# First sequence of an FNet + squared-ReLU kernel: E folded into Q's matmul group, small table loads on GpSimd's DMA queue, a new order of TensorE's opening

## The chip, the cores and the metric

The kernel runs on one core of a Trainium2 chip. The metric is the device time of one execution in microseconds (us); the number quoted for the kernel is the median of five runs, 1951.87 us (1948.48 to 1954.81). The profile is of one of these executions, whose own time is 1951.87 us and whose span, from the first to the last recorded instruction, is 1950.1 us.

## What is computed

Eight sequences of 3008 rows and 256 columns go through a two-dimensional Fourier transform of which only the real part is kept; the result, seen as 24064 tokens, goes through a small feed-forward block with a squared ReLU.

```python
X = np.fft.fft(x, axis=1)              # x: (8, 3008, 256) float32
X = np.fft.fft(X, axis=2)
t = X.real.astype(np.float32).reshape(8 * 3008, 256)
h = t @ w_in                           # w_in: (256, 2048)
r = np.maximum(h, 0.0)
out = (r * r) @ w_out                  # w_out: (2048, 256)
```

## The kernel before

**Two halves for each sequence.** For a sequence b the kernel first makes three matrices from the rows: P (128 x 1505, the cosine part of columns 0 to 127), Q (127 x 1505, the sine part of columns 1 to 127) and E (the cosine part of column 128, one row of 1505 values, which is wanted on all 128 partitions). Then, for blocks of 251 positions (`CK`) and for each of 8 steps j (`NJ`), `front` multiplies P by G1 and Q by G2 (L565, L566), adds E times a column gE and forms a sum and a difference on VectorE (L568 to L571), `combine` squares on ScalarE (L580, L581), and `back` multiplies by w_out (L605 or L618). G1, G2 and gE are products of the cosine and sine tables of the columns (`cosd`, `sind`) with w_in; `begin_win(j)` makes them for step j.

**How P, Q and E are made.** `load_x` brings seven tiles t of a sequence; `fold` adds and subtracts rows and columns on VectorE (`f_s`, `f_d`, `f_sc`, `f_dc`, `f_w`: L368 to L398), once for the cosine half (called `for_p`) and once for the sine half (`for_q`). `dft_ops` then has one group of five parts for each matrix and each parity kp of the output position: `even_n` (matmuls of tiles 0 to 3 into a tile of the pool `psd`, and a copy `da` on ScalarE, L475), `join_4` and `join_2` (VectorE, into `db` and `dc2`), `odd_n` (matmuls of tiles 4 to 6) and `join_1` (VectorE, into P, Q or E). Line L467 holds all these matmuls, L480 to L484 all the joins (the helper `both`). The pool `psd` has two buffers, and so has `psh`, which holds the first sequence's `odd_n` and later `front`'s products. The tables `cosT` and `sinT` are brought by `load_table` in 13 transfers each, of which ten are small (22 to 95 KB, the tiles 0 to 3) and three large (353 to 377 KB, the tiles 4 to 6).

**The first sequence (b = 0)** has no earlier work to hide in, so its order is written out by hand at L729 to L781: each call appends to the in-order queues of the engines. `groups_at` names the parts by number: P is 0 to 4 (kp 0) and 5 to 9 (kp 1), E is 10 to 14 and 15 to 19, Q is 20 to 24 and 25 to 29. For E, `even_n` and `odd_n` run the column broadcast to 128 columns, so that E comes out on all partitions at once. `awake(n)` issues n matmuls of the identity that nothing reads. `rounded(j)` is the last part of the conversion of w_in for step j (w_in comes as 64-bit numbers, which VectorE and ScalarE take apart: L241 to L254), `win[j][1]` the products into G1 and G2 (L269, L270), `win[j][2]` the matmul for gE (L278), and `copy_e` the copy into gE (L280).

**For the other sequences** E is computed once, in sequence 1's share of side work: seven rows, stored to the DRAM tile `e_dram` (L548) and read back by `load_e(b)`, broadcast over 128 partitions (L552).

**The DMA queues.** SyncE's queue (SP) issues nearly all transfers in program order; its rows in the trace are called SPq. Up to eight transfers are outstanding; an issue waits for the landing of the one eight before it, and for the instruction that frees or writes its buffer. ScalarE's queue issues three transfers, the tables `cosd` and `sind` (L739). GpSimd (POOL) issues none. In the main loop `weights()` appends for step i, among others, the load of w_in for step i + 3 (`begin_win(i + 3)`, whose transfers are issued by L226 on SP and whose first instruction on VectorE is L241).

Of the kernel before, what the change touches and what calls it, by code (L numbers as in the profile page):

```python
# [12 lines left out]
PSUM = bass.MemoryType.PSUM  # L13
P = 128
R = 32

# [63 lines left out]
def kernel(  # L82
# [12 lines left out]
    nc = tc.nc  # L95
# [72 lines left out]
    G2 = const.tile([P, F], F32, name="G2")  # L168
    gE = const.tile([P, NFC], F32, name="gE")

    def load_table(tab, src, tiles):

        for t in tiles:
            c, r0, step, rows = TILES[t]
            for i, (s0, count) in enumerate(row_tiles(S)):
                mine = [r for r in range(count) if (s0 + r - r0) % step == 0 and 0 <= (s0 + r - r0) // step < rows]
                if mine:
                    o, m = (s0 + mine[0] - r0) // step, len(mine)
                    while m % 15 and m % 16 and o + m < P and mine[0] + step * m < P:
                        m += 1  # L180
                    nk = NC[0][c]
                    nc.sync.dma_start(out=tab[o:o + m, :, PLACE[t]:PLACE[t] + nk],
                                     in_=src[mine[0]:mine[0] + step * (m - 1) + 1:step, :, i, 0:nk])

    make_identity(nc, ident)
    ramp = const.tile([P, 2], F32, name="ramp")
    nc.vector.memset(ramp[:, 0:1], 1151.0)
    nc.vector.memset(ramp[:, 1:2], 255.0 * 2.0 ** 23)
# [71 lines left out]
    def begin_win(j):  # L260

        w = ep.tile([P, 2, CH], F32, name="win", tag="sB" if j % 2 else "sA")
        finish = convert(parts(w, 1), win.pop(j, None) or load(pair_in(j)))

        def products():
            for tab, G, nm in ((cosd, G1, "mC"), (sind, G2, "mD")):
                pg = psm.tile([P, CH], F32, name="pg", tag=nm)
                for i in range(2):
                    nc.tensor.matmul(pg, tab[:, i], w[:, i], start=i == 0, stop=i == 1)  # L269
                nc.scalar.copy(G.rearrange("p (h j f) -> j p h f", h=2, j=NJ)[j],  # L270
                               pg.rearrange("p (h f) -> p h f", h=2))

        def for_e():

            ps = psd.tile([P, CH], F32, name="pe", tag="d")
            for h in range(2):
                fc = j + NJ * h
                nc.tensor.matmul(ps[:, h:h + 1], G2[:, fc * P:(fc + 1) * P], ident[:, P - 1:], start=True, stop=True)  # L278

            return lambda: nc.vector.tensor_scalar_mul(gE[:, j::NJ], ps[:, 0:2], 0.5)  # L280

        win[j] = finish, products, for_e
# [48 lines left out]
    NE = B - 1  # L331
    xe = const.tile([P, 4, NT, NE], F32, name="xe")
    we = const.tile([P, 2, NT, NE], F32, name="we")
    e_dram = dp.tile([NE, NKT], F32, name="e_dram")
    nc.gpsimd.memset(xe, 0.0)

    def load_column(t):
# [14 lines left out]
    def fold(b, t):  # L352
# [42 lines left out]
        def f_w(part=slice(0, D)):  # L395
            v, w = st["sc"], w_of(t)
            for kp in range(2):
                tt(out=w[r, kp, part], in0=v[r, 0, part], in1=v[r, 1, part], op=ALU.subtract if kp else ALU.add)  # L398

        if b == 0:  # L400
            return [f_s, f_d, f_sc, f_dc, lambda: f_w(PART[0]), lambda: f_w(PART[1])]
        ops = [(0.9, f_s), (0.9, f_d), (0.7, f_sc), (0.6, f_dc), (1.1, f_w)]
        if not odd or t == ODD0:
            return ops, None
# [42 lines left out]
    def dft_ops(b):  # L447
# [2 lines left out]

        def start():
            PQE[b] = [pq.tile([n, NKT], F32, name=nm, tag=nm)
                      for nm, n in (("Pt", P), ("Qt", P - 1), ("Et", P))]

        def group(kp, which):
            n = NE if b is None else P - 1 if which == 1 else P
            tab = sinT if which == 1 else cosT
            n2, _, n1, n0 = NC[kp]
            st = {}

            def product(ps, c):
                ts = [t for t in range(NT) if TILES[t][0] == c]
                for t in ts:
                    rows = TILES[t][3]
                    w = we[0:rows, kp, t] if b is None else folded[b, t][0:rows, kp, PART[which % 2]]
                    w = w[:, H:H + 1].to_broadcast([rows, n]) if which == 2 and b is not None else w[:, 0:n]
                    nc.tensor.matmul(ps, w, tab[0:rows, kp, PLACE[t]:PLACE[t] + NC[kp][c]],  # L467
                                     start=t == ts[0], stop=t == ts[-1])

            def even_n():  # L470
                st["ps"] = psd.tile([P, 512], F32, name="pd", tag="d")[0:n]
                a = st["a"] = hp.tile([P, 2 * P], F32, name="da", tag="da", bufs=2)[0:n]
                for c, at, nk in ((0, 0, n2), (1, n2, n2), (2, 2 * n2, n1)):
                    product(st["ps"][:, at:at + nk], c)
                nc.scalar.copy(a[:, 0:n2], st["ps"][:, 0:n2])  # L475

            def both(lo, hi, a, ps):

                nk, nh = a.shape[-1], hi.shape[-1]
                tt(out=lo, in0=a, in1=ps, op=ALU.add)  # L480
                if which == 1:
                    tt(out=hi[:, ::-1], in0=ps[:, 0:nh], in1=a[:, 0:nh], op=ALU.subtract)
                else:
                    tt(out=hi[:, ::-1], in0=a[:, 0:nh], in1=ps[:, 0:nh], op=ALU.subtract)  # L484
# [8 lines left out]
                st["c"] = hp.tile([P, NC[0][3]], F32, name="dc2", tag="dc2", bufs=2)[0:n, 0:n0]  # L493
                both(st["c"][:, 0:n1], st["c"][:, n1:n0], a, ps[:, 2 * n2:2 * n2 + n1])

            def odd_n():

                pool, tag = (psh, "h") if b == 0 else (psd, "d")
                ps = pool.tile([P, 512], F32, name="pd", tag=tag)[0:n]
                st["odd"] = ps[:, 0:n0]  # L500
                if not b:
                    return product(ps[:, 0:n0], 3)
                nq = (n0 + 2) // 2 if kp else (n0 + 1) // 2
# [25 lines left out]
                else:  # L529
                    tt(out=o[:, 1::2], in0=a[:, 1:nq], in1=ps[:, 1:nq], op=ALU.subtract)  # L530

            def join_1():
                dst = PQE[1][2][0:n] if b is None else PQE[b][which]
                nh = S // 8
                both(dst[:, kp:kp + 2 * n0 - 1:2], dst[:, M - kp - 2 * (nh - 1):M - kp + 1:2], st["c"],
                     st["odd"])

            ops = [(0.1, even_n), (0.4, join_4), (0.5, join_2), (0.1, odd_n), (0.8, join_1)]
            if b and kp:
                ops.insert(4, (0.5, join_odd))  # L540
            return ops

        ops = [] if b is None else [(0.0, start)]
        for which in (2,) if b is None else (0, 1) if b else (0, 2, 1):
            for kp in range(2):
                ops += group(kp, which)
        if b is None:
            ops.append((0.0, lambda: nc.sync.dma_start(out=e_dram[:, :], in_=PQE[1][2][0:NE])))  # L548
        return ops

    def load_e(b):
        nc.sync.dma_start(out=PQE[b][2], in_=e_dram[b - 1:b].to_broadcast([P, NKT]))  # L552


    def front(b, k0, n, j, between):
# [4 lines left out]
        for h in range(2):  # L560
            fc = j + NJ * h
            fs = slice(fc * P, (fc + 1) * P)
            ps = psh.tile([P, 2, CH], F32, name="ph", tag="h")
            hP, hQ = ps[:, 0, 0:n], ps[:, 1, 0:n]
            nc.tensor.matmul(hP, G1[:, fs], pt[:, ks], start=True, stop=True)  # L565
            nc.tensor.matmul(hQ, G2[0:P - 1, fs], qt[:, ks], start=True, stop=True)  # L566
            t = hp.tile([P, CK], F32, name="he", tag="he")[:, 0:n]
            nc.vector.scalar_tensor_tensor(out=t, in0=et[:, ks], scalar=gE[:, fc:fc + 1], in1=hP,  # L568
                                           op0=ALU.mult, op1=ALU.add)
            tt(out=g[:, h, 0, 0:n], in0=t, in1=hQ, op=ALU.add)  # L570
            tt(out=g[:, h, 1, 0:n][:, ::-1], in0=t, in1=hQ, op=ALU.subtract)  # L571
            between()
# [152 lines left out]
    def rounded(j):  # L725
        win[j][0]()
# [8 lines left out]
    for_p(1)  # L735
    begin_win(0)
    load_x(0, 2)
    for dst, src in ((cosd, cos_d), (sind[:, :, 0:P - 1], sin_d), (sind[:, :, P - 1:], alt_d)):
        nc.scalar.dma_start(out=dst, in_=src.rearrange("(c p) m -> p c m", p=P))  # L739
    load_x(0, 3)  # L740
    load_x(0, 4)
    load_table(cosT, cos_s, (0,))
    load_x(0, 5)
    load_table(cosT, cos_s, (1,))
    load_x(0, 6)
    load_table(cosT, cos_s, range(2, NT))
    load_table(sinT, sin_s, range(ODD0, NT))
    win[1] = load(pair_in(1))
    load_table(sinT, sin_s, range(ODD0))
    win[2] = load(pair_in(2))  # L750
    for_p(2)
    rounded(0)
    win[0][1]()
    awake(10)
    for_p(3)
    groups_at(0, 5)
    awake(12)
    for_q(1)
    for_p(4)
    for_p(5)  # L760
    for_q(2)
    for_p(6)
    groups_at(3, 8, 1, 2)
    for_q(4)
    groups_at(6, 7)
    for_q(5)
    groups_at(10, 15, 4)
    for_q(6)
    groups_at(9, 13, 18, 11, 12, 16, 17, 14)
    awake(4)  # L770
    groups_at(23)
    begin_win(1)
    groups_at(19, 28)
    copy_e = win[0][2]()
    for_q(3)
    groups_at(20, 25)
    awake(10)
    begin_win(2)
    rounded(1)
    groups_at(21, 22, 24, 26, 27, 29)  # L780
    copy_e()  # L781
    LAG = 2
    BLOCKS = [(k0, min(CK, NKT - k0)) for k0 in range(0, NKT, CK)]
    steps = [(b, k0, n, j) for b in range(B) for k0, n in BLOCKS for j in range(NJ)]
# [136 lines left out]
```

## Time and profile before

| | us |
|---|---|
| median of five runs (lowest to highest) | 1951.87 (1948.48 to 1954.81) |
| profiled execution | 1951.87 |
| its span | 1950.1 |
| TensorE (PE) busy in the span | 1937.2 (99%) |
| VectorE (DVE) busy | 1398.7 (72%) |
| GpSimd (POOL) busy | 1171.3 (60%) |
| ScalarE (ACT) busy | 924.3 (47%) |
| PE busy, first 68 us | 60.2 |
| PE busy, from 110 us to the end (1840 us) | 1835.1 |

Columns of the timeline: start and length in us, engine, line of the kernel, operation, tile written and tiles read, shape, number of records, and in brackets the idle time before it and what ended it. A matmul of float32 stands as two records. PEclk in a table of windows is the mean clock that the chip granted to TensorE, 1.00 being full. "Busy" for PE includes the time in which a matmul runs at a lower clock.

### The profile page before, as it was taken

Reading aid. Unit: us, or ns where it says so; the run is one execution under the profiler, and the core shown is the slowest. Engines: PE = TensorE matmul, PEld = TensorE weight load, DVE = VectorE, ACT = ScalarE, POOL = GpSimd, SP = SyncE. Lnnn points to the kernel's source line nnn. Section 1 sums busy time; section 2 is a strip of 40 time slices with the busy share of each in tenths; the row PEclk is TensorE's granted clock in tenths of the full one; section 3 lists DMA queues with packets and bytes.
Section 4 is the critical chain, followed back from the end, with each engine's and each line's share of the span. In section 5 each row is a group of like instructions: output and inputs, shape, how many; then the busy total and the mean of one; then the engine's idle time right before and its main releaser. Section 6 shows DMA issues by size and latency. Waiting matters only on the chain.

```text
span 1950.1 us, 27794 instructions
## 1 busy us (share of the span) xinstructions
PE 1937.2 (99%) x9296; PEld 1724.4 (88%) x9296; DVE 1398.7 (72%) x3442; ACT 924.3 (47%) x1068; POOL 1171.3 (60%) x1705
## 2 busy tenths in 40 slices
PE   8999999999999999999999999999999999999998
PEld 7888888888988889888988889888898888988887
DVE  8898967777677766777667776677767777655654
ACT  1754544455444544445444444444544454444443
POOL 0037746676567665666557665666756676566655
PEclk9999999999999999999999999999999999999999
DMA  7332102111011101111011100121002101100101
GB/s 210 98 45 52 33 10 53 33 27 29 14 45 35 39 16 27 41 35 33 12 35 38 44 19 11 37 53 28 20 13 54 33 11 22 25 13 12 22 11 22
DMA packets 145387, 68.90 MB, mean 35 GB/s; under 512 B 129049, under 2 KB 136156, under 8 KB 145243
## 3 DMA queue, kind: packets, MB, share of 16 engines
q1 hardware_dynamic: 144144, 66.60, 15.4%
q8 instruction: 73, 1.20, 0.2%
q10 hardware_dynamic: 1099, 0.52, 0.1%
q14 instruction: 71, 0.58, 0.1%
HBM read 42.39 MB, written 24.68 MB: 34 GB/s over the span
## 4 chain that ended last, share of the span: by engine, by line
PE 98%; DVE 1%; ACT 0%; DMA 0%; issue 0%; DVEq 0%
PE ph L565 17%; PE ph L566 17%; PE mC L618 16%; PE mA L618 16%; PE mB L618 16%; PE mD L618 8%; PE pd L467 3%; PE pd L514 2%; PE mB L605 1%; PE mA L605 1%; PE pg L269 1%; PE filled L195 1%; DMA xt<-in_x_dram 0%; PE pe L278 0%; DVE w L398 0%
## 5 line engine op out<-in xcount | busy, mean ns | idle before, releaser
L580 ACT ACTIVATE g<-g 128x1004 f32<-128x1004 f32 (+1 forms) x384 | 399.3, 1040 | 792.0 <-DVE g L571 444.9
L588 POOL TENSOR_TENSOR s<-g 128x251 f32<-128x251 f32 (+1 forms) x376 | 246.7, 656 | 711.2 <-ACT g L581 652.0
L568 DVE SCALAR_TENSOR_TENSOR he<-Et,gE,ph 128x251 f32<-128x251 f32 (+1 forms) x768 | 362.1, 472 | 415.2 <-PE ph L566 413.0
L565 PE MATMUL ph<-Pt,G 128*128 128x251 f32 (+1 forms) x1536 | 452.4, 375 | 0.0
L566 PE MATMUL ph<-Qt,G 127*128 127x251 f32 (+1 forms) x1536 | 452.2, 375 | 0.0
L581 ACT ACTIVATE g<-g 128x1004 f32<-128x1004 f32 (+1 forms) x384 | 399.3, 1040 | 12.2
L618 PE MATMUL mC<-s,wsum 128*128 128x251 f32 (+1 forms) x1504 | 381.4, 374 | 0.0
L618 PE MATMUL mA<-g,wout 128*128 128x251 f32 (+1 forms) x1504 | 379.9, 374 | 0.0
L570 DVE TENSOR_TENSOR g<-he,ph 128x251 f32<-128x251 f32 (+1 forms) x768 | 320.6, 417 | 55.6 <-POOL s L588 1.4
L566 PEld LDWEIGHTS ph<-Qt,G 127*128 127x128 f32 x1536 | 291.8, 190 | 36.1
L565 PEld LDWEIGHTS ph<-Pt,G 128*128 128x128 f32 x1536 | 288.2, 189 | 35.1 <-DVE g L571 0.8
L618 PEld LDWEIGHTS mC<-s,wsum 128*128 128x128 f32 x1504 | 285.5, 190 | 34.6
L618 PEld LDWEIGHTS mA<-g,wout 128*128 128x128 f32 x1504 | 282.9, 189 | 35.8 <-issue 1.3
L571 DVE TENSOR_TENSOR g<-he,ph 128x251 f32<-128x251 f32 (+1 forms) x768 | 314.3, 409 | 0.0
L590 POOL TENSOR_TENSOR s<-g 128x251 f32<-128x251 f32 (+1 forms) x376 | 305.3, 812 | 0.0
L589 POOL TENSOR_TENSOR s<-s,g 128x251 f32<-128x251 f32 (+1 forms) x376 | 274.7, 731 | 29.5
L591 POOL TENSOR_TENSOR s<-g,s 128x251 f32<-128x251 f32 (+1 forms) x376 | 253.8, 675 | 0.0
L618 PE MATMUL mB<-g,wsum 128*128 128x251 f32 (+1 forms) x752 | 220.5, 374 | 0.0
L618 PE MATMUL mD<-s,wout 128*128 128x251 f32 (+1 forms) x752 | 220.3, 374 | 0.0
L618 PE MATMUL mB<-s,wout 128*128 128x251 f32 (+1 forms) x752 | 219.9, 374 | 0.0
L618 PEld LDWEIGHTS mB<-g,wsum 128*128 128x128 f32 x752 | 142.6, 190 | 17.4
L618 PEld LDWEIGHTS mD<-s,wout 128*128 128x128 f32 x752 | 141.9, 189 | 17.7
(120 smaller groups left out, 1315.4 us busy)
## 6 DMA issues: line engine op xcount, KB each, us to landing
out_dram<-os SPq DMA_DIRECT2D x376, 56.0 KB
xt<-in_x_dram SPq DMA_DIRECT2D x32, 384.0 KB
xt<-in_x_dram SPq DMA_DIRECT2D x42, 128.0 KB
Et<-e_dram SPq DMA_DIRECT2D x7, 752.5 KB
xt<-in_x_dram SPq DMA_DIRECT2D x9, 512.0 KB
out_dram<-os SPq DMA_DIRECT2D x288, 6.8 KB
raw<-in_moe_w_in_dram SPq DMA_DIRECT2D x16, 256.0 KB
raw<-in_moe_w_out_dram SPq DMA_DIRECT2D x16, 256.0 KB
```

Of the source, the lines that this page charges most:

```text
L565: nc.tensor.matmul(hP, G1[:, fs], pt[:, ks], start=True, stop=True)
L566: nc.tensor.matmul(hQ, G2[0:P - 1, fs], qt[:, ks], start=True, stop=True)
L568: nc.vector.scalar_tensor_tensor(out=t, in0=et[:, ks], scalar=gE[:, fc:fc + 1], in1=hP, op0=ALU.mult, op1=ALU.add)
L570: tt(out=g[:, h, 0, 0:n], in0=t, in1=hQ, op=ALU.add)
L571: tt(out=g[:, h, 1, 0:n][:, ::-1], in0=t, in1=hQ, op=ALU.subtract)
L580: act(v, v, AF.Relu)
L581: act(v, v, AF.Square)
L588: gt(out=s1, in0=g21, in1=g22, op=ALU.add)
L589: gt(out=s2, in0=s1, in1=g11, op=ALU.subtract)
L590: gt(out=s3, in0=g11, in1=g21, op=ALU.subtract)
L591: gt(out=s4, in0=g12, in1=s2, op=ALU.subtract)
L618: nc.tensor.matmul(acc[nm][:, i, 0:n], w, v[:, 0:n], start=j == 0 and i == 0, stop=j == NJ - 1, skip_group_check=True)
```

## The change

1. **E becomes row 127 of Q.** For the first sequence Q's tile has 128 rows in place of 127. ScalarE copies the folded column 128 of each tile, with a sign, into the last column of a zeroed 128 x 128 matrix (`f_e`, into `lone`, which borrows `wsum`'s memory). These matrices are multiplied by the cosine tables into the same PSUM tile into which Q's sine products then accumulate (`even_e`, `odd_e`; Q's own parts start without clearing). The joins of Q for b = 0 take a sign for each partition (`signs`: the last row is joined as cosine, the others as sine) in a `scalar_tensor_tensor` in place of a `tensor_tensor`. E's own two groups, their ten parts, are gone.
2. **E is spread again.** `spread_e` takes the first 251 positions by a matmul with the last column of the identity and a copy on ScalarE. `spread_rest` stores row 127 of Q to `e_dram` and loads positions 251 to 1504 back, broadcast: two transfers on SP, issued ahead of the main loop's.
3. **Small loads on GpSimd's queue.** The ten small transfers of `cosT` and the three of `cosd` and `sind` are issued by GpSimd, after an instruction on GpSimd (`after`) that reads the first tile of x; the ten small transfers of `sinT` follow after a second such instruction, which reads the last large transfer of `cosT`. SP issues the seven x tiles first and then the large transfers.
4. **A new order of the opening.** E's even matmuls stand ahead of P's odd ones; the products of w_in for step 0 move from the front to behind P's odd matmuls; 36 of the 84 `awake` matmuls are left out (the first 48 stay). New numbers of the parts: Q is now 10 to 17 (kp 0) and 18 to 25 (kp 1), in the order `even_n`, `join_4`, `join_2`, `odd_n`, `join_lo`, `even_e`, `odd_e`, `join_hi`.

```diff
+    def after(ap, i):
+        nc.gpsimd.tensor_copy(gate[:, i:i + 1], ap)
-                    nc.sync.dma_start(out=tab[o:o + m, :, PLACE[t]:PLACE[t] + nk],
+                    queue.dma_start(out=tab[o:o + m, :, PLACE[t]:PLACE[t] + nk],
...
+    lone = wsum.rearrange("p a j h -> p (a j) h")
+    nc.gpsimd.memset(lone[:, 0:2 * NT], 0.0)
...
+        def f_e():
+            nc.scalar.mul(lone[r, 2 * t:2 * t + 2, P - 1:], w_of(t)[r, :, H:H + 1], -1.0 if TILES[t][0] else 1.0)
...
+            def even_e():
+                st["ps"] = psd.tile([P, 512], F32, name="pd", tag="d")
+                for c, at, nk in EVEN:
+                    product(st["ps"][:, at:at + nk], c, True)
...
+                if both_in:
+                    join = nc.vector.scalar_tensor_tensor
+                    if only != 1:
+                        join(out=lo, in0=ps, scalar=signs[:, 0:1], in1=a, op0=ALU.mult, op1=ALU.add)
+                    if only != 0:
+                        join(out=hi[:, ::-1], in0=a[:, 0:nh], scalar=signs[:, 1:2], in1=ps[:, 0:nh],
+                             op0=ALU.mult, op1=ALU.add)
+                    return
...
+                pool, tag = (psd, "d") if b != 0 else (psm, "mA") if kp == 0 and both_in else (psh, "h")
...
+    def spread_e():
+        _, qt, et = PQE[0]
+        ps = psd.tile([P, CH], F32, name="pe", tag="d")[:, 0:CK]
+        nc.tensor.matmul(ps, last.to_broadcast([P, P]), qt[:, 0:CK], start=True, stop=True)
+        nc.scalar.copy(et[:, 0:CK], ps)
+    def spread_rest():
+        _, qt, et = PQE[0]
+        nc.sync.dma_start(out=e_dram[0:1], in_=qt[P - 1:P])
+        nc.sync.dma_start(out=et[:, CK:], in_=e_dram[0:1, CK:].to_broadcast([P, NKT - CK]))
...
+    after(xt[0, 0][0:1, 0, 0:1], 0)
+    load_table(cosT, cos_s, range(ODD0), nc.gpsimd)
     for dst, src in ((cosd, cos_d), (sind[:, :, 0:P - 1], sin_d), (sind[:, :, P - 1:], alt_d)):
-        nc.scalar.dma_start(out=dst, in_=src.rearrange("(c p) m -> p c m", p=P))
+        nc.gpsimd.dma_start(out=dst, in_=src.rearrange("(c p) m -> p c m", p=P))
+    for t in range(4, NT):
+        load_x(0, t)
+    load_table(cosT, cos_s, range(ODD0, NT))
     load_table(sinT, sin_s, range(ODD0, NT))
+    after(cosT[0:1, 0, PLACE[NT - 1]:PLACE[NT - 1] + 1], 1)
+    load_table(sinT, sin_s, range(ODD0), nc.gpsimd)
...
     rounded(0)
-    win[0][1]()
-    awake(10)
     for_p(3)
-    groups_at(0, 5)
-    awake(12)
+    groups_at(0, 5, 15, 23)
     for_q(1)
...
-    groups_at(3, 8, 1, 2)
+    groups_at(3, 8)
+    win[0][1]()
+    groups_at(1, 2)
     for_q(4)
     groups_at(6, 7)
     for_q(5)
-    groups_at(10, 15, 4)
+    groups_at(4, 16, 24)
     for_q(6)
-    groups_at(9, 13, 18, 11, 12, 16, 17, 14)
-    awake(4)
-    groups_at(23)
+    groups_at(13, 21, 9)
+    copy_e = win[0][2]()
     begin_win(1)
-    groups_at(19, 28)
-    copy_e = win[0][2]()
     for_q(3)
-    groups_at(20, 25)
-    awake(10)
+    groups_at(10, 18)
+    rounded(1)
     begin_win(2)
-    rounded(1)
-    groups_at(21, 22, 24, 26, 27, 29)
+    groups_at(11, 12, 14, 19, 20, 22)
+    spread_e()
+    groups_at(17, 25)
     copy_e()
+    spread_rest()
```

## The prediction, made before the changed kernel ran

> **What bounds the kernel now.** I read the page's head first, then windows of 2 us over the first 68 us, then the timelines of TensorE, VectorE and SP there.
>
> ```profile
> span 1950.1 us, 27794 instructions
> PE 1937.2 (99%) x9296; PEld 1724.4 (88%) x9296; DVE 1398.7 (72%) x3442; ACT 924.3 (47%) x1068; POOL 1171.3 (60%) x1705
> ```
>
> TensorE has no room after the opening: from 110 us on it is busy for 1835.1 of 1840 us, with matmuls that the change leaves alone. So the end moves by as much as the point moves from which TensorE runs without a gap and at full clock. In the windows (columns: PE, PEld, DVE, ACT, POOL busy, clock, DMA share, GB/s) that point is near 68 us:
>
> ```profile
> 42.00:44.00 2.00, 0.48 (x3) 0.22 (x3) 1.31 (x5) 0.24 (x1) 0.00 (x0) 0.97 0.24 90
> 44.00:46.00 2.00, 2.00 (x8) 2.00 (x9) 0.73 (x2) 0.00 (x0) 0.00 (x0) 0.50 0.00 0
> 50.00:52.00 2.00, 2.00 (x11) 1.79 (x10) 0.44 (x1) 0.00 (x0) 0.00 (x0) 0.83 0.00 0
> 58.00:60.00 2.00, 0.70 (x4) 0.27 (x2) 1.97 (x7) 1.97 (x3) 0.00 (x0) 1.00 0.00 0
> 60.00:62.00 2.00, 1.10 (x5) 1.10 (x6) 1.93 (x4) 1.97 (x5) 0.00 (x0) 0.73 0.00 0
> 66.00:68.00 2.00, 2.00 (x6) 1.56 (x6) 1.97 (x6) 1.10 (x2) 0.00 (x0) 0.56 0.30 116
> ```
>
> The clock falls to 0.50 twice, after a TensorE gap of 1.5 us and after one of 2.2 us. From the means, it is low from 43.9 to 50.7 and from 60.9 to 67.8, so 6.8 us each time, about 6.9 us from where work resumes. TensorE's own rows:
>
> ```profile
> 21.27 2.34 PE L467 MATMUL pd<-cosT,w 95*128 95x95 f32 x16
> 26.13 9.95 PE L467 MATMUL pd<-cosT,w 128*128 128x377 f32 x40
> 40.98 1.33 PE L467 MATMUL pd<-sinT,w 95*127 95x95 f32 x8
> 43.84 2.41 PE L467 MATMUL pd<-sinT,w 95*127 95x94 f32 x8 [1.52 <-DVE dc L482]
> 46.04 4.47 PE L195 MATMUL filled<-ident 128*128 128x128 f32 x20
> 60.90 1.01 PE L278 MATMUL pe<-ident,G 128*128 128x1 f32 x4 [2.20 <-ACT G L270]
> ```
>
> Two even parts (both kp) cost 2.2 us at full clock; P odd, E even and E odd together 9.8, so an odd pair costs 3.8. VectorE's marks are these:
>
> ```profile
> 23.91 0.34 DVE L484 TENSOR_TENSOR dc<-db,pd 128x188 f32<-128x188 f32 x1
> 26.46 0.34 DVE L484 TENSOR_TENSOR dc<-db,pd 128x188 f32<-128x188 f32 x1
> 42.62 0.25 DVE L480 TENSOR_TENSOR db<-da,pd 127x95 f32<-127x95 f32 x1 [1.32 <-ACT da L475]
> 48.12 0.54 DVE L482 TENSOR_TENSOR Qt<-pd,dc 127x376 f32<-127x376 f32 x1
> 51.56 0.48 DVE L568 SCALAR_TENSOR_TENSOR he<-Et,gE,ph 128x251 f32<-128x251 f32 x1 [2.83 <-PE ph L566]
> 55.82 0.42 DVE L241 TENSOR_SCALAR fd<-raw 128x512 uint32<-128x512 uint32 x1
> ```
>
> P's two `join_2` end at 24.2 and 26.8, Q is complete at 48.66, the first `he` is 4.26 us ahead of the L241 of w_in 3. That L241 heads the chain VectorE, ScalarE (conversion, square of step 0, copies of G), TensorE at 60.90: 5.08 us. On SP the load of w_in 3 was out long before:
>
> ```profile
> 32.42 2.52 SPq L226 DMA_DIRECT2D raw<-in_moe_w_in_dram  x4
> 35.04 1.55 SPq L226 DMA_DIRECT2D raw<-in_moe_w_out_dram  x2
> 257.25 0.27 SPq L548 DMA_DIRECT2D e_dram<-Et  x1
> 300.00 0.36 SPq L552 DMA_DIRECT2D Et<-e_dram  x1
> ```
>
> **The opening up to P's odd matmuls.** VectorE's order up to 26.8 is unchanged, and in the trace it runs from 4.55 without waiting for a transfer; I keep 24.2 and 26.8. The two `signs` instructions fall into its idle first 4 us. GpSimd's zeroing of `lone` (1792 columns) costs about 1.6 us, by `xe` (196 columns, 0.26) against `ident` (128 columns, 0.20), and is over by 3.3 us; the first reader behind it comes at 5.3.
>
> *Transfers on GpSimd.* The trace has none. Bounds for one issue: 0.43 us (SP's median for `cosT`) and 1.35 (SP's longest, for `sinT`); I take the middle, 0.9, since GpSimd's rows (656 to 812 ns for 128x251) are longer than VectorE's (409 to 417). The first goes at 4.6, the tenth is out at 13.6 and lands about 2 us later (the 41 KB store at 257.25 took 1.65): 15.6, or 20.1 by the upper bound. P even, ready on VectorE's side at 15.3, has to be done by 22.9 for the join at 23.2, and needs 1.2 us for kp 0: the margin is 6 us, or 1.6. The ten of `sinT` wait for the last large `cosT`: some 5.4 MB up to there, at the 270 GB/s that the stretch from 2 to 26 us moves, give 21.6; they end at 21.6 + 9 + 2 = 32.6 (37.1 by the upper bound), and Q even takes them after 40. So the queue move costs nothing if one issue stays below 1.5 us. It gains nothing either: VectorE's order, not a load, sets 24.2.
>
> [...]
>
> *VectorE beside GpSimd.* A 128x512 `tensor_tensor` takes 683 to 685 ns in the first 40 us, with GpSimd idle, and 857 to 867 between 115 and 240, with GpSimd computing: 25% more. Thirteen issues of 0.9 us beside it cost 0 to 2.9 us. I take 0, as the nearest rows, memsets on both engines around 1 us, show no stretching, and keep 2.9.
>
> *E even ahead of P odd.* E even needs both `psd` buffers, which `join_2` frees at 24.2 and 26.8. After P even ends (near 18) nothing is left for TensorE, since the 22 `awake` in this stretch and w_in 0's products have gone: a gap of some 6 us. By the two gaps above the clock falls. E even runs 24.2 to 26.4 and 26.8 to 29.0 at half speed, and P odd starts at 29.0 where it started at 26.3. The low clock ends 6.9 us after work resumes: 31.1 counted from 24.2, 33.7 counted from 26.8. I take 33.7, as both measured stretches kept it through pieces of small matmuls. P odd does 2.35 of its 3.81 us until then and ends at 35.15.
>
> [...]
>
> **From there to Q.** TensorE now has no gap: w_in 0's products 1.73 (eight records, as at 73.8), E odd 3.81, Q odd 3.81, gE 0.34, Q even kp 0 1.2: 46.05, where it was 42.33. VectorE has 3.8 us less to do (E's twelve joins, between 31.7 and 37.0) and waits. Q's joins: 0.29 to the first, then twelve at twice 2.07 = 4.15 (kp 1's matmuls end at 47.25, in time). As `scalar_tensor_tensor` each costs 0 to 0.06 more (475 against 418 ns on the same shape), so 0 to 0.7; I take 0.35. Q is complete at 50.85, against 48.66.
>
> **The new wait on SP.** Its store of Q's row waits for that, its load for the store; behind both stand w_in 3, w_out 0, w_in 4 and w_out 1, which went out at 33 to 38. The store: 1.65 us (257.25 until its bytes end at 258.9). The load: 3.2 for all 1505 columns, 1.0 of it ahead of the first byte, so 2.8 for 1254. w_in 3: 1.9 behind it (its 524 KB at 62.4 to 64.3). Together 6.4 (5.9 to 7.4 with semaphores): L241 at 57.25, against 55.82. The other path, `spread_e`, one block of `front` and 4.26 us, reaches it at 55.5 and is hidden. w_out 0 lands 1.9 us after w_in 3 and is read 3.26 after L241, so nothing else is late; the other 1254 columns of E are wanted only in the second block.
>
> **The rest.** TensorE resumes 5.08 us after L241, at 62.3, cold as before. If the low stretch is a half shorter, 1.7 us are won; I take 0. The 36 `awake` that go free no time by themselves, except the ten at 46.04, whose end (50.5) held back `front`; that gain is inside the hidden path. Sum: 57.25 - 55.82 = +1.4 us, on the profiled execution's 1951.87, which is also the median: 1953.3. Its own range: -1.3 (clock back at 31.1), -0.35, -1.7 and -0.5, so 1949.5; +2.9, +0.35 and +1.0, so 1957.5.
>
> **Rivals.**
> - *The clock holds.* If TensorE is warm from 24 on, P odd ends at 31.7, 3.45 us sooner, L241 comes at 53.8, and a cold stretch after it that is halved or gone saves 1.7 to 3.4: 1951.87 - 2.0 - 2.6 = 1947.3. For it: the gap of 2.28 us at 14.7 lowered nothing. Against: the gap here is twice as long.
> - *The software queue is late.* From 1.5 us an issue on, P's joins and all of VectorE behind them slip by ten times the excess; `sinT`'s second batch, behind thirteen first ones, reaches Q even from 1.8 on. At 2.0: 4.6 + 20 + 2 = 26.6 for `cosT` is 5 late, `sinT` at 30.6 + 22 = 52.6 another 2.6: 1953.3 + 7.6 = 1960.9. For it: no row prices such an issue. Against: it needs half as much again as SP's longest.
> - *The late w_in 3 does not matter*, since the conversions run ahead: then the hidden path decides, 55.5, and the time is 1951.6. Against: L241 stands in order before the second `front`.
>
> **How the numbers follow.** About 0.2%, 3.9 us, is what a measurement of this kernel can tell from no change: bounds 1948.0 and 1955.8. Forecast 0.50 (0.31 within, 0.19 slower, as its range passes the bound by 1.7 and contention is unpriced); clock holds 0.27 (0.22 faster, 0.05 within); late queue 0.17 (slower); w_in 3 harmless 0.06 (0.05 within, 0.01 faster). Faster 0.23, within 0.41, slower 0.36. The range, 1946.8 to 1959.5, takes in most of the clock rival and the cheaper half of the late queue.
>
> **What would show it.** Right: clock 0.5 between about 23 and 33 us; P odd from 29; SP waiting on Q's last join, and VectorE's L241 of w_in 3 ended by its transfer, near 57. Wrong: GpSimd's issues above 1.5 us with VectorE waiting on P even; a clock of 1.00 from 24 to 36; w_in 3 there before VectorE asks.

## The result and the profile after

The changed kernel takes 1955.08 us (median of 31 runs, 1953.13 to 1956.73); the kernel before, in runs beside it, 1951.14 (median of 55). The ratio is 1.0017, 95% interval 1.0013 to 1.0022: some 3.3 us slower (3.9 by the medians). The profiled execution, 1953.13 us with a span of 1951.4, is the quickest of the 31, so the profile shows 1.3 us of the loss. What can be said of the rest comes with the runs c_dve, c_pe and a2_early below.

TensorE's rows in the timeline of the changed kernel:

```profile
14.72 0.86 PE L494 MATMUL pd<-cosT,w 95*128 95x95 f32 x4
16.77 0.56 PE L494 MATMUL pd<-cosT,w 96*128 96x189 f32 x2 [1.19 <-DMA cosT<-in_cos_s_dram]
20.03 2.78 PE L494 MATMUL pd<-cosT,w 92*128 92x189 f32 x10 [2.70 <-DMA cosT<-in_cos_s_dram]
24.34 5.00 PE L494 MATMUL pd<-cosT,wsum 95*128 95x95 f32 x16 [1.54 <-DVE dc L530]
29.14 4.68 PE L494 MATMUL pd<-cosT,w 128*128 128x377 f32 x12
43.36 2.42 PE L494 MATMUL pd<-sinT,w 95*127 95x95 f32 x16
62.09 0.61 PE L295 MATMUL pe<-ident,G 128*128 128x1 f32 x4 [1.73 <-ACT G L287]
```

P's even half comes in three pieces, the second and the third behind waits of 1.19 and 2.70 us for a small table. E's even half (the matrix `wsum`, 24.34) then waits 1.54 us for VectorE's join `dc`, and P's odd half starts only at 29.14, against some 26.3 before. From there to the end of Q's even half (45.8) TensorE has no gap. Its clock, in the windows of 2 us of the same kernel (columns: PE, PEld, DVE, ACT, POOL busy, clock, DMA share, GB/s):

```profile
18.00:20.00 2.00, 0.00 (x0) 0.00 (x1) 1.93 (x7) 0.00 (x0) 0.00 (x0) 1.00 1.08 314
20.00:22.00 2.00, 1.97 (x9) 2.00 (x10) 1.93 (x6) 0.24 (x1) 0.00 (x0) 0.59 1.06 237
28.00:30.00 2.00, 2.00 (x7) 1.71 (x7) 0.34 (x2) 0.00 (x0) 0.42 (x1) 0.50 1.06 284
30.00:32.00 2.00, 2.00 (x6) 1.15 (x6) 0.04 (x1) 0.00 (x0) 1.12 (x2) 0.85 0.26 49
46.00:48.00 2.00, 0.00 (x0) 0.00 (x0) 1.93 (x6) 1.94 (x4) 0.00 (x0) 0.91 0.00 0
54.00:56.00 2.00, 1.76 (x7) 1.13 (x6) 1.94 (x4) 0.58 (x2) 0.00 (x0) 0.88 0.87 258
60.00:62.00 2.00, 0.36 (x2) 0.00 (x0) 2.00 (x6) 1.97 (x5) 0.00 (x0) 1.00 0.30 112
62.00:64.00 2.00, 1.91 (x11) 1.77 (x12) 1.93 (x5) 1.97 (x5) 0.00 (x0) 1.00 0.11 19
```

It is halved from about 20.4 to 30.6 us, 10.2 us in all (of the window at 20 a mean of 0.59 leaves 1.64 us at 0.50, of that at 30 a mean of 0.85 leaves 0.6), while the last part of P's even half, E's even half and part of P's odd half run. A second low stretch goes from 47.6 to 54.5, by the same working. From there on the clock is full, where the kernel before had it halved from 60.9 to 67.8. VectorE's marks:

```profile
31.96 0.55 DVE L526 TENSOR_TENSOR Pt<-dc,pd 128x377 f32<-128x377 f32 x1 [3.62 <-PE pd L494]
45.00 0.32 DVE L521 SCALAR_TENSOR_TENSOR db<-pd,signs,da 128x95 f32<-128x95 f32 x1 [4.69 <-ACT da L512]
48.72 1.12 DVE L523 SCALAR_TENSOR_TENSOR Qt<-dc,signs,pd 128x376 f32<-128x376 f32 x2
51.89 0.48 DVE L643 SCALAR_TENSOR_TENSOR he<-Et,gE,ph 128x251 f32<-128x251 f32 x1 [1.99 <-PE ph L641]
57.00 0.43 DVE L258 TENSOR_SCALAR fd<-raw 128x512 uint32<-128x512 uint32 x1 [0.31 <-DMA raw<-in_moe_w_in_dram]
```

L258 is the old L241, the first instruction on w_in. VectorE waits 3.62 us for P's odd half; Q is complete at 49.84; the L258 of w_in 3 starts at 57.00, against 55.82. The queues of GpSimd and SP:

```profile
5.18 4.77 POOL L189 DMA_DIRECT2D cosT<-in_cos_s_dram  x8
12.48 1.24 POOL L189 DMA_DIRECT2D cosT<-in_cos_s_dram  x2 [2.53 <-DMA cosT<-in_cos_s_dram]
49.86 0.26 SPq L623 DMA_DIRECT2D e_dram<-Qt  x1
51.60 1.57 SPq L243 DMA_DIRECT2D raw<-in_moe_w_in_dram  x2
```

GpSimd issues a transfer in 0.60 us, and after eight of them waits 2.53 us until one has landed. SP holds w_in 3 behind Q until 51.60.

### The profile page after: what moved, and what is told of

Read it like the earlier page. It is cut to its first block, busy times and chain, and to the rows that moved or that the text cites. A ratio compares the mean times of both kernels' runs of the same rounds, so it can differ in the third digit from the quotient of the medians.

```text
span 1951.4 us, 27655 instructions
## 1 busy us (share of the span) xinstructions
PE 1931.8 (99%) x9226; PEld 1716.1 (88%) x9226; DVE 1395.3 (72%) x3432; ACT 924.8 (47%) x1074; POOL 1187.1 (61%) x1731
## 4 chain that ended last, share of the span: by engine, by line
PE 95%; DVE 4%; DMA 1%; issue 0%; SPq 0%; ACT 0%; DVEq 0%
PE ph L641 16%; PE ph L640 16%; PE mC L693 16%; PE mA L693 16%; PE mB L693 16%; PE mD L693 8%; PE pd L494 3%; PE pd L569 2%; DVE w L415 0%; DVE m L270 0%; DVE he L643 0%; DVE fd L268 0%; DVE g L646 0%; PE mA L680 0%; PE mB L680 0%
```

## The experiments

One number joins all runs: the span minus the start of w_in 3's L258 (L241). It is 1950.1 - 55.82 = 1894.3 before and 1951.4 - 57.00 = 1894.4 after. What moves this instruction moves the end: the difference stays within 0.7 us in all runs but d_conv, c_dve and c_pe, whose edits change the steps around it. But for the two single runs, each median is of 7 to 12 executions, and each ratio is to executions of the kernel before taken beside them. The medians come in part from different chips, so across groups the ratios are the safer comparison.

| run | edit | us, median | ratio to before, 95% | L258 at | span - L258 |
|---|---|---|---|---|---|
| a1_warm | many fillers | 1956.50 | 1.0029 [1.0020, 1.0039] | 60.66 | 1894.2 |
| a2_early | w_in 3 loaded ahead of SP's wait | 1954.44 | 1.0014 [1.0005, 1.0023] | 58.69 | 1894.2 |
| a3_warm_early | both | 1955.46 | 1.0020 [1.0011, 1.0029] | 59.45 | 1894.4 |
| a4_sync | small tables back on SP | 1957.15 | 1.0028 [1.0017, 1.0038] | 60.97 | 1894.4 |
| a5_podd | P odd ahead of E even | 1950.05 | 0.9989 [0.9980, 0.9998] | 52.74 | 1894.3 |
| b1_warm | fewer fillers | 1951.77 | 1.0002 [0.9993, 1.0010] | 56.78 | 1893.8 |
| b2_podd | P odd first, fillers | 1950.22 | 0.9986 [0.9968, 1.0004] | 53.97 | 1893.7 |
| b3_podd_early | and the early load | 1947.60 | 0.9979 [0.9970, 0.9987] | 51.03 | 1893.8 |
| d_conv | and a conversion moved | 1947.53 | 0.9978 [0.9968, 0.9989] | 49.77 | 1895.6 |
| e_before_warm | before, 7 fillers | 1949.54 | 0.9984 [0.9975, 0.9993] | 52.58 | 1894.2 |
| c_dve | after, VectorE loaded | 1958.88 (one run) | | 59.29 | 1897.8 |
| c_pe | after, TensorE loaded | 1957.96 (one run) | | 59.34 | 1896.9 |

**Fillers, too many (a1_warm).**

```diff
-    groups_at(0, 5, 15, 23)
+    awake(40)
+    groups_at(0, 5)
+    awake(14)
+    groups_at(15)
+    awake(10)
+    groups_at(23)
...
+    awake(24)
     spread_e()
```

> The changed kernel plus 88 dummy matmuls of the identity in TensorE's new gaps (40 ahead of P even, 14 and 10 around E even of kp 0, 24 ahead of the spreading of E); nothing else. Theory CLOCK (the low clock from 20 to 30.5 us and again from 47.6 sets when Q is done): clock 1.00 from 7 to 60, P odd done near 31.7 instead of 33.7, Q done near 47.8 instead of 49.75, L258 of w_in 3 near 55.0 instead of 57.0 (held by SP from there), time 2 us below the changed kernel: about 1953. Theory SP (the queued load of w_in 3 decides): Q's end moves the load too, so also about -2, but VectorE then waits over 2 us for w_in 3. Theory QUEUE (GpSimd's late table loads decide): no gain, 1955.

The fillers were too many: one takes 0.22 us (two records of 0.11), so the first 40 pushed P's even half back. From TensorE's timeline of this run:

```profile
13.78 10.10 PE L212 MATMUL filled<-ident 128*128 128x128 f32 x89
23.71 2.34 PE L494 MATMUL pd<-cosT,w 95*128 95x95 f32 x16
33.43 3.97 PE L494 MATMUL pd<-cosT,w 128*128 128x377 f32 x12
```

The clock was full here (P's odd half takes 3.97 us against 4.68 in the changed kernel; the mean over the run is 0.999), and yet P's odd half started 4.3 us later than in the changed kernel. Nothing follows for or against the clock.

**The load of w_in 3 ahead of SP's wait, alone and with those fillers (a2_early, a3_warm_early).**

```diff
     copy_e()
+    win[3] = load(pair_in(3))
     spread_rest()
```

> The changed kernel with the load of w_in 3 issued just ahead of the store and load of E on SP; nothing else. Theory SP: L258 of w_in 3 no longer waits, 2 us or more gained: 1953. Theory CLOCK: in the changed kernel's trace VectorE arrives at that load only 0.3 us before it lands, so 0.3 us: 1954.8. Theory QUEUE: 1955.

> Both edits: 88 dummy matmuls and the early load of w_in 3. Theory CLOCK: first he near 48.2, L258 of w_in 3 near 52.6 instead of 57.0; the stage from there to about 101 us is VectorE's own chain (44.2 us from L258 to the last conversion), so the end moves by the same 4.4 us: 1950.7. If instead TensorE bounds that stage, the gain is smaller, about 2 us: 1953. Theory QUEUE: 1955.

In neither does L258 wait for its transfer: it follows the first `he` at 4.26 us (54.43 and 58.69 in a2_early). The gain over the changed kernel, 0.0017 against 0.0014, lies within the intervals; a3_warm_early gains 1.0 on a1_warm, where L258 waited 0.23 us, again with overlapping intervals. This fits a changed kernel in which SP's wait is nearly level with the path through `spread_e` and `front`.

**The small tables back on SP, `cosd` and `sind` on ScalarE's queue (a4_sync).**

```diff
-    after(xt[0, 0][0:1, 0, 0:1], 0)
-    load_table(cosT, cos_s, range(ODD0), nc.gpsimd)
+    load_table(cosT, cos_s, range(ODD0))
...
-    after(cosT[0:1, 0, PLACE[NT - 1]:PLACE[NT - 1] + 1], 1)
-    load_table(sinT, sin_s, range(ODD0), nc.gpsimd)
     win[1] = load(pair_in(1))
+    load_table(sinT, sin_s, range(ODD0))
```

> The changed kernel with the small table loads back on SP (in the place in the program where GpSimd has them) and cosd, sind on ScalarE's queue, without the two gate copies. Theory QUEUE: cosT's small tables land before 20.0, P even starts earlier, and the time falls by 2 us or more: 1953. Theory CLOCK: VectorE's order sets the join at 23.1 in any case, so within 1 us of 1955.1; it can be later instead, if the large tables now queue behind the small ones and P odd waits for them.

P's even half now runs early; E's even half still has to wait for the join, and the wait is one piece:

```profile
16.34 1.65 PE L494 MATMUL pd<-cosT,w 92*128 92x189 f32 x10 [0.34 <-DVE w L415]
26.25 5.00 PE L494 MATMUL pd<-cosT,wsum 95*128 95x95 f32 x16 [8.26 <-DVE dc L530]
31.04 5.81 PE L494 MATMUL pd<-cosT,w 128*128 128x377 f32 x12
```

VectorE meanwhile waits 0.44 and 0.87 us for tiles of x, which stand behind the small tables on SP here. Put back in this place, the small tables do not win the time back. That GpSimd's queue is not what made the kernel slower follows from a5_podd below, which keeps it and is no slower than before.

**Fewer fillers (b1_warm).**

```diff
-    groups_at(0, 5, 15, 23)
+    awake(20)
+    groups_at(0, 5)
+    awake(9)
+    groups_at(15)
+    awake(5)
+    groups_at(23)
...
+    awake(12)
     spread_e()
```

> The changed kernel with filler matmuls of 0.22 us each where TensorE waits: 20 ahead of P's even half, 9 and 5 around E's even half, 12 ahead of the constant row. They are fewer than in the first trial, whose fillers pushed the work behind them. Clock theory (the half clock from 20.3 to 30.5 and from 47.6 to 54.4 us is what the change costs): granted clock 1.0 throughout, P's odd half done at 31.6 us against 33.8, Q complete near 47.7 against 49.75, the first conversion instruction of w_in 3 (L258) no longer waits for VectorE's chain but for its transfer, which the wait of SP for Q holds back, and starts near 55.0; VectorE waits there some 2 us. The span is 1894.3 longer than that: 1949.3 us, the time near 1951.0. Rival (the joins and the later E are the price, the clock is not): span as after, 1951.4 or more.

The time is level with before, and the fillers are the only edit: by the medians they win the 3 us back. That the low clock is all of this is not shown, since the profiles have only 0.8 us of it (spans of 1951.4 and 1950.6). In the opening the windows show 0.50 for about 3.4 us (21.4 to 24.8) in place of 10.2, and none from 47.6 to 54.5. P's odd half starts no earlier (29.05 against 29.14), as fillers stand before it, but runs 0.7 us faster. Q is complete 0.8 us earlier than in the changed kernel, at 49.04; L258 comes 0.2 us earlier, since now the transfer decides. VectorE's row in this run:

```profile
56.78 0.43 DVE L258 TENSOR_SCALAR fd<-raw 128x512 uint32<-128x512 uint32 x1 [2.69 <-DMA raw<-in_moe_w_in_dram]
```

**P's odd half ahead of E's even half, and nothing else (a5_podd).**

```diff
-    groups_at(0, 5, 15, 23)
+    groups_at(0, 5)
...
-    groups_at(3, 8)
+    groups_at(3, 8, 15, 23)
```

> One part of the change undone, and nothing else: P's odd half ahead of E's even half on TensorE, no filler added. If that order is a price of the change: P's odd half starts near 23 instead of 29.1 us without waiting for E's buffers, TensorE is not idle for those 1.5 us, Q is complete about 1.5 us earlier (48.2 against 49.75) when the low clock lasts as long, L258 of w_in 3 comes 7.3 to 8.1 us after it, at 55.5 to 56.3, and the span is 1949.8 to 1950.6: level with before. If only the missing fillers count (the low clock): no more than 0.5 us from the changed kernel's 1955.1.

This one move takes 5.0 us off the changed kernel by the medians (5.5 by the ratios, 4.4 between the profiles), more than expected, and puts it just below before. TensorE and its clock in this run:

```profile
19.84 7.13 PE L494 MATMUL pd<-cosT,w 92*128 92x189 f32 x22 [2.55 <-DVE sc L401]
26.81 2.34 PE L494 MATMUL pd<-cosT,wsum 95*128 95x95 f32 x16
```

```profile
20.00:22.00 2.00, 2.00 (x10) 2.00 (x10) 1.93 (x7) 0.24 (x1) 0.00 (x0) 0.65 1.07 237
22.00:24.00 2.00, 2.00 (x5) 1.12 (x5) 1.90 (x7) 0.64 (x4) 0.64 (x2) 0.50 1.07 320
24.00:26.00 2.00, 2.00 (x8) 1.24 (x7) 1.93 (x6) 0.00 (x0) 2.00 (x5) 1.00 1.09 262
```

P's odd half follows its even half without a pause, and the clock is back at 24.0 us, where the changed kernel had it low until 30.6. When E's turn comes, at 26.81, VectorE has freed its first buffer (the join `dc` is done at 24.51), and the second follows at 27.07, ahead of the second half of E's matmuls.

The two timelines can be set side by side from the start of the last part of P's even half (20.03 and 19.84) to w_in 0's products (33.66 and 28.99). The changed kernel is 4.67 us later at the end of this stretch. The wait for E's buffers is 1.54 of them, E's even half at half clock 2.62 (4.80 us from start to start against 2.18), the rest of P 0.32, and the later start 0.19.

**The same with fillers, and with the early load (b2_podd, b3_podd_early).**

```diff
-    groups_at(0, 5, 15, 23)
+    awake(20)
+    groups_at(0, 5)
+    awake(6)
...
-    groups_at(3, 8)
+    groups_at(3, 8, 15, 23)
...
+    awake(12)
     spread_e()
...
+    win[3] = load(pair_in(3))
     spread_rest()
```

The last line is in b3_podd_early alone.

> P's odd half back ahead of E's even half on TensorE, 20 fillers of 0.22 us ahead of the first matmuls, 6 between P's odd half and E's even half, 12 ahead of the constant row. If putting E's even half ahead of P's odd half is a cost of the change: P's odd half at 23.4 to 28.1 us, Q's even half ends near 41.5, Q complete near 45.6, L258 of w_in 3 near 52.9 behind its transfer (SP's wait), span 1947.2, time near 1949, faster than before. If E's even half merely moves (TensorE does the same work in another order and Q's odd half waits for the sine table anyway): Q complete no earlier than in the run with fillers alone, span 1949 to 1951.5.

> The run before with the load of w_in 3 issued ahead of SP's wait for Q. If SP's wait is what the freed time runs into: VectorE finds w_in 3 landed, L258 of it starts right after the first step's joins, near 50.7 us, span 1945.0, time near 1946.8. If the load was hidden anyway: same as the run before within 0.3 us.

With P's odd half first, fillers add nothing to the time (1950.22 against 1950.05): in both, Q is done by 46 us and L258 waits for its transfer (2.92 and 1.20 us). Taking SP's wait away then gives 2.6 us by the medians (1.4 by the ratios, 2.9 between the profiles):

```profile
46.77 0.48 DVE L643 SCALAR_TENSOR_TENSOR he<-Et,gE,ph 128x251 f32<-128x251 f32 x1 [0.65 <-PE ph L641]
51.03 0.42 DVE L258 TENSOR_SCALAR fd<-raw 128x512 uint32<-128x512 uint32 x1
```

So the new wait on SP, hardly felt in the changed kernel, is the next bound as soon as Q comes earlier. This version beats both kernels.

**The kernel before with seven fillers in its gap (e_before_warm).**

```diff
-    groups_at(20, 25)
+    groups_at(20)
+    awake(7)
+    groups_at(25)
     awake(10)
```

> The kernel before with seven filler matmuls of 0.22 us in the one stretch where its TensorE sits idle (42.3 to 43.84 us), after which its clock is halved from 43.9 to 50.7. If that low clock is a cost of before too: clock 1.0 there, its ten fillers after it take 2.2 instead of 4.47 us, the first step's joins start near 48.8 instead of 51.56, L241 of w_in 3 near 53.0 instead of 55.82, span 1947.3 against 1950.1. If something else holds w_in 3 back there: span 1950 as before.

As expected: clock 1.00 in every window from 14 to 66 us, L241 at 52.58, 2.5 us gained. The rows of its TensorE:

```profile
42.19 1.72 PE L195 MATMUL filled<-ident 128*128 128x128 f32 x14
43.88 1.32 PE L467 MATMUL pd<-sinT,w 95*127 95x94 f32 x8
45.03 2.39 PE L195 MATMUL filled<-ident 128*128 128x128 f32 x20
```

The kernel before thus had a low clock of its own to lose. Its other executions point the same way: of the 24 taken beside this run, the seven with a mean clock of 0.999 have a median of 1950.06 us, the five with 0.995 one of 1953.99. So b3_podd_early is fairly compared with this run: 1949.54 to 1947.60, 1.9 us by the medians and 1.0 by the ratios (0.9984 and 0.9979), whose intervals overlap. What the change is worth, with P's odd half first, fillers and the early load added to it, against a kernel before that has its fillers too, is thus 1 to 2 us, and not separated from nothing.

**A conversion moved into VectorE's idle stretch, on top of b3_podd_early (d_conv).**

```diff
+    rounded(1)
+    begin_win(2)
     groups_at(10, 18)
-    rounded(1)
-    begin_win(2)
+    rounded(2)
...
-        if i + 2 < NJ:
+        if 2 < i + 2 < NJ:
             rounded(i + 2)
```

> The fastest version so far (P's odd half first, fillers, early load of w_in 3) with the end of w_in 2's conversion (L268, L270, L271: 2.0 us) moved from behind the first step's joins into VectorE's idle stretch ahead of Q's joins (36.5 to 41.2 us). L258 of w_in 3 then starts near 49.1 instead of 51.0. If TensorE follows at once the span falls by 2.0 to 1942.8; if the second step's product, ready near 51.3, is what VectorE then waits for, by only 0.7 to 1944.1.

No gain (1947.53 against 1947.60, run on different chips). VectorE now waits 0.51 and 0.80 us for TensorE in the second step, whose first `he` starts 4.55 us after that of the first step instead of 5.20. Those 0.65 us are cancelled in the profile by a first `he` that comes 0.67 later (47.44); whether they exist in the mean stays open.

**What paces the steps after L258 (c_dve, c_pe).** Each does one operation twice in `front`, in the steps 1 to 6 of the first pass and for h = 0; the outputs stay the same. The first repeats the `he` join on VectorE, the second the first product on TensorE:

```diff
+            for _ in range(2 if b == 0 and k0 == 0 and h == 0 and 0 < j < NJ - 1 else 1):
                 nc.vector.scalar_tensor_tensor(out=t, in0=et[:, ks], scalar=gE[:, fc:fc + 1], in1=hP,
                                                op0=ALU.mult, op1=ALU.add)
```

```diff
+            for _ in range(2 if b == 0 and k0 == 0 and h == 0 and 0 < j < NJ - 1 else 1):
                 nc.tensor.matmul(hP, G1[:, fs], pt[:, ks], start=True, stop=True)
```

> The changed kernel with one more VectorE instruction of 0.47 us in each of the steps 1 to 6 of the first pass (the first he join, L643, is done twice), 2.8 us in all, all behind L258 of w_in 3. If VectorE paces these steps: span minus the start of L258 of w_in 3 is 1894.3 + 2.8 = 1897.1 us. If TensorE paces them: 1894.3, unchanged within 0.5.

> The changed kernel with one more TensorE matmul of 0.39 us in each of the steps 1 to 6 of the first pass (the first ph product, L640, is done twice), 2.4 us in all, all behind L258 of w_in 3; the counterpart of the run with six more VectorE instructions. If VectorE paces these steps: span minus the start of L258 of w_in 3 stays at 1893.8 to 1894.4. If TensorE paces them: 1896.7.

The load on VectorE comes out in full (1897.8, +3.4 for 3.1 us: a pair of joins takes 0.99 us against 0.47; ahead of the first pair VectorE also waits 0.57 us for TensorE). But so does the load on TensorE (1896.9), where VectorE paced by itself should have shown nothing. In c_pe the clock was low from 64.5 to 71.3 us as well (means of 0.56 from 64 to 68 and 0.59 from 68 to 72), and VectorE waits 0.34 us at 69.87 and 0.96 us at 77.49 for TensorE's products. The runs, one execution each, fit a VectorE that paces these steps with a TensorE that has little to spare: a low stretch of 6.8 us fits in (before: low from 60.9 to 67.8, 1894.3; e_before_warm: no low stretch up to 66 us, 1894.2), and a low stretch with 2.4 us more does not. What the load would cost at full clock wasn't measured.

The trace of c_dve shows one thing more. Up to 57 us it is the changed kernel, and its clock (same columns as above) is low from 20.0 to 33.7, 13.6 us in all, 3.4 us longer than in the profiled run:

```profile
20.00:22.00 2.00, 0.21 (x2) 0.00 (x0) 1.90 (x7) 0.00 (x0) 0.00 (x0) 0.51 1.11 249
32.00:34.00 2.00, 2.00 (x5) 1.19 (x4) 0.00 (x0) 0.00 (x0) 0.03 (x1) 0.58 0.64 132
34.00:36.00 2.00, 2.00 (x8) 1.14 (x7) 1.39 (x3) 0.00 (x0) 1.20 (x2) 1.00 0.22 54
```

The same length, 13.6 us, stands in c_pe (20.1 to 33.7) and a2_early (20.4 to 34.1), which share this opening. In these three P's odd half starts at 29.93 to 31.35 and L258 at 58.69 to 59.34, 1.7 to 2.3 us later than in the profiled run. The clock is not all of it. VectorE comes to P's first join 0.79 (c_pe), 1.58 (a2_early) and 2.21 us (c_dve) later than in the profiled run, and P's odd half starts later by just as much. VectorE had been held up, for the most part, by tiles of x, in c_pe by the first, in the two others by a later one too; in the profiled run it gets the first at 4.50 and waits for none after that. In this order (c_pe, a2_early, c_dve):

```profile
5.11 0.69 DVE L385 TENSOR_TENSOR fs<-xt 95x512 f32<-95x512 f32 x1 [3.40 <-DMA xt<-in_x_dram]
11.66 0.69 DVE L385 TENSOR_TENSOR fs<-xt 96x512 f32<-96x512 f32 x1 [1.52 <-DMA xt<-in_x_dram]
12.31 0.69 DVE L385 TENSOR_TENSOR fs<-xt 96x512 f32<-96x512 f32 x1 [1.25 <-DMA xt<-in_x_dram]
```

Under the longer low clock P's odd half then takes 5.12 to 5.85 us instead of 4.68. Together this has the size of the step from 1953.13 to the median, 1955.08, but that the 30 executions without a profile went the same way is not shown. Nor is it shown that the change's new order of loads is what makes x late: the two traces with the old order (before and e_before_warm) have no wait for x after the first tile, and two are few.

## Why the prediction was right, and where it wasn't

The forecast was 1953.3 us; the profiled execution has 1953.13, the median 1955.08. The path that decides was told rightly: L258, held by its transfer behind SP's wait, at 57.00 (forecast 57.25). That the profiled execution comes so near is in part luck. Q came 1.0 us early, and the chain of transfers from Q to L258 took 7.16 us where 6.4 was taken (with 7.4 as its bound), and these two errors nearly cancel. And this execution is the quickest of 31; the usual one is 1.8 us above the forecast. Point by point, by its steps:

- **GpSimd's queue.** An issue takes 0.60 us, between the bounds 0.43 and 1.35 and below the 0.9 taken; the folds on VectorE beside them stretch by nothing (0.67 to 0.69 us for L385 and L389, as before). The wait after the eighth issue (2.53 us), told in the text for SP and not applied to GpSimd, made up for the short issues: the tenth was out at 13.7, forecast 13.6. The landing was mis-sized: 2 us were taken after the issue, and the median for `cosT`'s small tables was 6.6 to 7.3 us, so that the last wait for `cosT` ended at 20.03, near the upper bound (forecast 15.6 to 20.1). The DMA share was 0.95 to 1.08 while they were under way; for `sinT`, issued from 24 to 32 us while the share fell from 1.09 to 0.26, the median from issue to landing was 2.4 to 6.3 us. What made the landings late, the trace does not show.
- **"The margin is 6 us, or 1.6."** It was used up but for 0.1 us. The late pieces put the gap, and the fall of the clock, near 20.3 instead of after P even; P even's second part then ran at half speed, 2.78 us for ten records, and ended at 22.8 against the 22.9 allowed. It cost nothing: VectorE does not wait at the joins of P's even half (L526 and L530, from 23.14 to 26.75), here or in a2_early, c_pe and c_dve.
- **"I keep 24.2 and 26.8."** Right in the profiled run. In a2_early, c_pe and c_dve VectorE waits for x, and its joins come 0.8 to 2.2 us later. The sum had no term for this, and its range has none either.
- **E even ahead of P odd.** Right: P odd from 29.14 (forecast 29.0) at a halved clock. a5_podd shows that this order is the price of the change, and that the price is higher than the whole loss of 1.4 us in the sum: undoing it takes 5 us off. The sum set it against a kernel before whose own low clock it took as given.
- **The end of the low clock.** 33.7 was taken, with 31.1 as the bound: 30.6 in the profiled run, 33.7 in c_dve and c_pe, 34.1 in a2_early. Both ends occur: low for 10.2 us in the one, for 13.6 in the three.
- **Q.** Complete at 49.84, forecast 50.85; the earlier end of the low clock is the difference. The joins came out at the dear end of their price: 0.30 against 0.25 us for the small ones and 0.61 against 0.55 for the large.
- **The new wait on SP.** L258 at 57.00, forecast 57.25, ended by its transfer as the list of signs said, but with a wait of only 0.31 us: the path called hidden at 55.5 ended at 56.69, because `spread_e` and `front` ran at half clock from 47.6 to 54.5 (1.04 to 1.05 us a product of `front`, against 0.59 from 57.2 on), and the text had no low stretch there. a2_early fits two paths that are level.
- **"The end moves by as much as the point from which TensorE runs without a gap and at full clock."** This reading of the profile was wrong. TensorE was at full clock from 54.5 on after, and at half clock until 67.8 before, with the same distance from L258 to the end. A shorter low stretch behind L258, which the sum offered as a gain of up to 1.7 us, shows no gain here.
- **The rivals.** *The clock holds*, 1947.3, was overpriced: with the clock held but for 3.4 us of the opening, b1_warm has 1951.77. By that same reading 2.6 us of its gain fall away; Q is complete at 49.04, not 47.4, as the fillers stand before P's odd half; and the transfers behind Q take 7.7 us, not 6.4. *The software queue is late* fell by its price, 0.60 against 1.5 us an issue. *The late w_in 3 does not matter* was nearly true in the changed kernel, and false in the faster versions that keep SP's order (b1_warm, a5_podd, b2_podd: waits of 1.20 to 2.92 us).

## What to carry to other kernels

When a step is moved ahead of another on an in-order engine, ask what its buffers wait for: E's even half was ready to be issued early, but it needed two buffers of `psd`, which VectorE's joins freed only at 24.20 and 26.75, and P's odd half, which needed neither, queued behind it until 29.14. A busy share of 99% over the whole span does not say which engine paces a stage: find one instruction whose distance to the end is the same in every run, and explain that. Compare a change with a version of the old kernel from which the same waste has been removed, or the gain of one is taken for that of the other.

## What was not expected of the hardware

- By the windows of these runs TensorE's clock lay low for 3.4 us (b1_warm from 21.4, a5_podd from 20.6), 6.8 (before from 43.9 and from 60.9, the changed kernel from 47.6, c_pe from 64.5), 10.2 (the changed kernel from 20.4) or 13.6 us (a2_early, c_dve, c_pe). With the same opening of the program it was 10.2 us in one execution and 13.6 in three others; in those VectorE had also waited for x, and the two go together with an L258 1.7 to 2.3 us later.
- A filler matmul of 128x128 in float32 takes 0.22 us at full clock (20 records, ten matmuls, in 2.39 us) and 0.45 at half clock (4.47 us), so fillers put in to keep the clock up must be counted as work.
